# The output layer of a second feed-forward network as Strassen's seven products, with every weight factor streamed from DRAM

## Chip, core and metric

One core of a Trainium2 chip runs the whole program. The metric is device time in microseconds (us); less is better. Times are medians of several executions, and one execution of the kernel before was also profiled.

## What is computed

Three stages follow each other on 2304 tokens (4 batches of 576).

```python
# masked attention, 8 heads of 64: x is [2304, 512]
# first network
h = maximum(maximum(x @ w1, x @ w2), x @ w3)      # [2304, 768]
x2 = h @ w_out                                    # [2304, 512]
# second network
h = x2 @ w_in                                     # [2304, 2048]
g = maximum(h, 0) + alpha * minimum(h, 0)
out = g @ moe2_w_out                              # [2304, 512]
```

The matrix products of the two networks are done in three passes: each operand is split into a high and a low part of a shorter float type, and high x high, high x low and low x high are added up (the table `PAIRS`). So every product below stands for three matmuls.

## The kernel before

**The weave (0 to 324 us).** For batches 0 to 2, attention, the first network and the preparation of weights are tasks with a position; a list scheduler (`Weave.run`) puts them in order by estimated costs. Weights arrive as 64-bit numbers: `from_double` fetches a chunk, a ScalarE and two VectorE instructions (`rebase_words`, `join_words`) make a 32-bit word of it, `split_tasks` makes the two parts. `pair_tasks` does this for eight pairs q of the second network's input weights, forms Strassen's sums of a pair on VectorE (L484) and stores four factor tiles per pair in DRAM. Four chunks of the output weights are prepared and stored there too (`out_chunk_tasks`).

**The last batch of the first network (324 to 400 us)** is written out unit by unit (`first_net`): 36 gate units of 12 matmuls, 8 output units of 18. Beside it `Converter` prepares the other twelve chunks of output weights directly, `load_x2` brings the activations of block 0 back from DRAM, and four of their seven factors are split (`split_x2`).

**The second network (400 us to the end).** The tokens stand in three blocks of 768. A block takes eight steps n, one per pair q. In a step `h_products` computes the pair's hidden values by Strassen's seven products of 6 matmuls with 384 columns each (L814). Two PSUM banks, `ph`, take the products in turn, so a product can start only when VectorE (L819) or ScalarE (L831) has read the one two places ahead of it. `hidden` applies the slope alpha on VectorE (L793, L795) and splits the result (L798 on ScalarE, L801 on VectorE). Between the products stand the output matmuls of the step before: `o_units` yields twelve units of three matmuls with 512 columns (L773), one or two behind each product. They add up in six banks `po` over all 16 chunks. All 16 chunks of output weights stay in SBUF (the pool `wp`); only the input factors (`load_pair`, four tiles per step) come from DRAM. At the block's end `po` is copied and stored. The next block's activations are loaded in step 4 and their factors computed on POOL (L676, L197).

All transfers are issued in program order on one queue, SyncE's (SP). Each engine works its instructions off in the order written.

Of the kernel before, what the change touches and what calls it, by code (L numbers as in the profile page):

```python
# [17 lines left out]
DM = 512  # L18
# [21 lines left out]
DIRECT = 12  # L40
DIRECT_STEPS = tuple(range(4, 28, 2))
LOAD_X, SPLIT_X = 20, 36
# [106 lines left out]
def attention_maxout_prelu_kernel(  # L149
# [59 lines left out]
    od = [dram.tile([P, 2, DM], F32, name=f"wo{f}") for f in range(NF2)]  # L209

    wp = pool(ctx, "wp", NF2)
    wp1 = pool(hx, "wp1", 3 * NF1 + NF1 - NF2)
# [242 lines left out]
    def store_tasks(key, ak, view, n, place, pos, given=None):  # L455

        sk = ("wst", key)
        split_tasks(key, ak, view, n, lambda: wst.tile([P, 2, DM], F32R, tag="w", name="w"), pos,
                    makes=[("wst", sk)], given=given)
        add(load(n), lambda _: nc.sync.dma_start(place[:, :, :n], tl["split", key][:, :, :n].bitcast(F32)),  # L460
            pos, needs=[key], gives=[("stored", key)], uses=[sk])
# [5 lines left out]
    def pair_tasks(q, pos, pace):  # L467
        ek, ok = (from_double(("in", f), w2[f, 0], pos + pace * (f - 2 * q), pace,
                              [("sums", q - 2)] if q > 1 else ())
                  for f in (2 * q, 2 * q + 1))  # L470
        half = DM // 2
        sk = [("word", "sum", q, i) for i in range(2)]
        late = pos + pace

        def sums(_):
            e, a = (tl[k].bitcast(F32) for k in (ek, ok))
            for k in sk:
                tl[k] = words_p.tile([P, DM], U32, tag="word", name="word")
            c, d = (tl[k].bitcast(F32) for k in sk)
            for out_, x, y, op in ((c[:, :half], e[:, :half], a[:, :half], ALU.subtract),  # L480
                                   (a[:, :half], a[:, :half], a[:, half:], ALU.add),
                                   (c[:, half:], a[:, :half], e[:, :half], ALU.subtract),
                                   (d[:, :half], e[:, half:], c[:, half:], ALU.subtract)):
                nc.vector.tensor_tensor(out=out_, in0=x, in1=y, op=op)  # L484

        def whole(a):
            return a

        store_tasks(("h", q, 0), ek, whole, DM, hd[q][0], pos)
        add((dve(half, 4),), sums, late, needs=[ek, ok], gives=[("sums", q)],  # L490
            makes=[("word", k) for k in sk], uses=[ek, ok])
        for i, (k, n) in enumerate(((ok, DM), (sk[0], DM), (sk[1], half))):
            store_tasks(("h", q, i + 1), k, whole if n == DM else lambda a: a[:, :half], n,
                        hd[q][i + 1], late, given=("sums", q))

    def out_chunk_tasks(f, pos, pace):
        ak = from_double(("out", f), w2[f, 1], pos, pace, [("sums", NQ - 1)])
        store_tasks(("o", f), ak, lambda a: a, DM, od[f], pos)

    class Converter:  # L500


        def __init__(self, blocks, raws, floats):
            self.blocks, self.raws, self.floats = list(blocks), raws, floats
            self.sources = [src for src, _ in self.blocks]
            self.fetched, self.line = [], []

        def fetch(self, n=1):
            for src in self.sources[:n]:
                raw = self.raws.tile([P, DM, 2], U32, tag="raw", name="raw")  # L510
                nc.sync.dma_start(raw.rearrange("p n t -> p (n t)"), src.bitcast(U32))
                self.fetched.append(raw)
            del self.sources[:n]

        def steps(self, raw, key):
            a = self.floats.tile([P, DM], U32, tag="word", name="word")
            rebase_words(raw, a)
            yield True
            join_words(raw, a)
            self.fetch()  # L520
            yield True
            t = words[key] = wp.tile([P, 2, DM], F32R, tag="w", name="w")
            nc.scalar.copy(t[:, 0], a.bitcast(F32))
            yield True
            sub(t[:, 1], a.bitcast(F32), t[:, 0].bitcast(F32))

        def step(self, n=1):

            for _ in range(min(n, len(self.blocks))):
                self.line.append(self.steps(self.fetched.pop(0), self.blocks.pop(0)[1]))  # L530
            self.line = [block for block in self.line if next(block, False)]
# [132 lines left out]
    EARLY_X = 4  # L664
    xs, x2h = {}, {}

    def load_x2(blk):

        for i in range(2):
            t = xsp.tile([P, 2, 2, HB], F32, tag="xs", name="xs")  # L670
            for h in range(2):
                nc.sync.dma_start(t[:, :, h, :], x2d[2 * blk + h][:, i::2, :])
            b11, b12, b21, b22 = t[:, 0, 0], t[:, 0, 1], t[:, 1, 0], t[:, 1, 1]
            t2, t3, t4 = (tsp.tile([P, HB], F32, tag="t", name="t") for _ in range(3))
            for out_, x, y in ((t3, b22, b12), (b12, b12, b11), (t2, b22, b12), (t4, b21, t2)):
                nc.gpsimd.tensor_tensor(out=out_, in0=x, in1=y, op=ALU.subtract)  # L676
            for name, x in (("11", b11), ("T1", b12), ("21", b21), ("22", b22), ("T2", t2),
                            ("T3", t3), ("T4", t4)):
                xs[blk, name, i] = x

    def split_x2(blk, k):

        name = PRODUCTS[k][1]
        for i in range(2):
            t = (xmp if k < EARLY_X else xmp1).tile([P, 2, HB], F32R, tag=f"x{k}{i}", name=f"x{k}{i}")
            split(t[:, 0], t[:, 1], xs.pop((blk, name, i)), nc.scalar,
                  nc.gpsimd if blk else nc.vector)
            x2h[blk, k, i] = t

    def load_pair(n):  # L690

        for i in range(4):
            t = words["h", n, i] = (hw1 if n % 3 == 2 else hw).tile([P, 2, DM], F32R, tag="w", name="w")
            m = DM if i < 3 else DM // 2
            nc.sync.dma_start(t[:, :, :m].bitcast(F32), hd[n % NQ][i][:, :, :m])

    def load_out_chunk(f):
        t = words["o", f] = wp.tile([P, 2, DM], F32R, tag="w", name="w")
        nc.sync.dma_start(t.bitcast(F32), od[f])
# [55 lines left out]
    hw1 = pool(ctx, "hw1", 4)  # L755
    xmp1 = pool(ctx, "xmp1", 1)
    gp = pool(ctx, "gp", 8)
    cp = pool(ctx, "cp", 8)
    osp = pool(ctx, "osp", 2)
    ps_h = ctx.enter_context(tc.tile_pool(name="ps_h", bufs=2, space=PSUM, reuse_waits="tile"))  # L760
    ps_o = ctx.enter_context(tc.tile_pool(name="ps_o", bufs=6, space=PSUM, reuse_waits="tile"))
    gts, accs = {}, {}

    def o_unit(n, j, t, first, last):

        blk, q = divmod(n, NQ)
# [8 lines left out]
        if q == NQ - 1 and last:  # L775
            osb = osp.tile([P, DM], F32, tag="osb", name="osb")
# [162 lines left out]
```

## Time and profile before

| | |
|---|---|
| median of 3 runs | 784.21 us (783.13 to 785.36) |
| the profiled execution | 785.25 us, its span 783.5 us |
| TensorE matmul busy, of the span | 760.6 us (97%) |
| VectorE, ScalarE, POOL | 514.6 (66%), 320.5 (41%), 63.1 us (8%) |
| mean granted TensorE clock | 0.992 of full speed |
| bytes moved by DMA | 122.68 MB, mean 157 GB/s |

The span is the time from the first to the last event of the trace. Busy time of matmuls includes overlap of neighbours, so the pace is read from the distance between starts. Of a group of instructions in the timeline the start of the first, the time to the end of the last and the count are given.

### The profile page before, as it was taken

Reading aid. Unit: us, or ns where it says so; the run is one execution under the profiler, and the core shown is the slowest. Engines: PE = TensorE matmul, PEld = TensorE weight load, DVE = VectorE, ACT = ScalarE, POOL = GpSimd, SP = SyncE. Lnnn points to the kernel's source line nnn. Section 1 sums busy time; section 2 is a strip of 40 time slices with the busy share of each in tenths; the row PEclk is TensorE's granted clock in tenths of the full one; section 3 lists DMA queues with packets and bytes.
Section 4 is the critical chain, followed back from the end, with each engine's and each line's share of the span. In section 5 each row is a group of like instructions: output and inputs, shape, how many; then the busy total and the mean of one; then the engine's idle time right before and its main releaser. Section 6 shows DMA issues by size and latency. Waiting matters only on the chain.

```text
span 783.5 us, 13813 instructions
## 1 busy us (share of the span) xinstructions
PE 760.6 (97%) x5056; PEld 705.2 (90%) x5056; DVE 514.6 (66%) x1419; ACT 320.5 (41%) x952; POOL 63.1 (8%) x68
## 2 busy tenths in 40 slices
PE   5899998999999999999999999999999999999997
PEld 4689898999999999999988989998999899989996
DVE  4898998779756243167656677586657677666563
ACT  5997796657755254244421111143111124111112
POOL 1000000000000000002200030071004034000000
PEclk9899999999999999999999999999999999999999
DMA  7577668876761010467363464326454432634002
GB/s 237 156 229 243 213 240 289 284 273 233 265 215 61 1 36 17 151 246 245 111 210 110 126 199 133 94 95 220 144 160 140 120 131 92 211 118 131 1 0 82
DMA packets 51636, 122.68 MB, mean 157 GB/s; under 512 B 7280, under 2 KB 22640, under 8 KB 51568
## 3 DMA queue, kind: packets, MB, share of 16 engines
q1 hardware_dynamic: 51568, 121.79, 46.7%
q8 instruction: 40, 0.66, 0.4%
q14 instruction: 28, 0.23, 0.1%
HBM read 95.56 MB, written 26.21 MB: 155 GB/s over the span
## 4 chain that ended last, share of the span: by engine, by line
PE 84%; DVE 6%; ACT 4%; DMA 4%; issue 1%; SPq 0%; DVEq 0%; ACTq 0%
PE po L773 25%; PE bank L543 22%; PE ph L814 22%; PE bank L565 9%; PE bank L302 2%; PE bank L368 2%; DMA raw<-in_w 2%; PE bank L343 2%; DVE word L431 1%; ACT e L317 1%; DVE word L429 1%; DVE e L310 1%; DMA k<-in_kTs 1%; ACT word L425 1%; DVE w L238 1%
## 5 line engine op out<-in xcount | busy, mean ns | idle before, releaser
L543 PE MATMUL bank<-x,w 128*128 128x288 f32 x1728 | 235.4, 296 | 3.1 <-DVE x L238 2.2
L543 PEld LDWEIGHTS bank<-x,w 128*128 128x128 f32 x1728 | 230.3, 189 | 4.9 <-DVE x L238 2.4
L773 PE MATMUL po<-w,g 128*128 128x512 f32 x864 | 224.8, 392 | 0.0
L814 PE MATMUL ph<-x,w 128*128 128x384 f32 x1008 | 204.1, 337 | 1.3 <-DVE c L819 0.6
L814 PEld LDWEIGHTS ph<-x,w 128*128 128x128 f32 x1008 | 180.5, 188 | 16.8 <-DVE c L819 2.1
L773 PEld LDWEIGHTS po<-w,g 128*128 128x128 f32 x864 | 160.0, 188 | 23.0
L798 ACT CAST g<-neg 128x384 fp32r<-128x384 f32 x96 | 49.4, 514 | 246.1 <-DVE neg L795 246.0
L819 DVE TENSOR_TENSOR c<-ph,c 128x384 f32<-128x384 f32 x168 | 91.1, 554 | 84.3 <-PE ph L814 83.9
L565 PE MATMUL bank<-h,w 128*128 128x288 f32 x576 | 79.5, 297 | 0.0
L801 DVE TENSOR_TENSOR g<-neg,g 128x384 fp32r<-128x384 f32 x96 | 55.3, 576 | 35.0 <-ACT g L798 34.0
L565 PEld LDWEIGHTS bank<-h,w 128*128 128x128 f32 x576 | 76.8, 188 | 1.2 <-issue 0.2
L317 ACT ACTIVATE e<-e,nm 96x128 f32<-96x128 f32 (+2 forms) x176 | 67.8, 392 | 8.6 <-DVE nm L310 8.6
L795 DVE SCALAR_TENSOR_TENSOR neg<-c,neg 128x384 f32<-128x384 f32 x96 | 62.0, 646 | 3.3
L632 DVE TENSOR_TENSOR t<-bank,t 128x288 f32<-128x288 f32 x72 | 32.5, 452 | 37.2 <-PE bank L543 33.7
L238 DVE TENSOR_TENSOR w<-word,w 128x512 fp32r<-128x512 f32 x72 | 47.7, 664 | 13.8 <-ACT w L235 12.2
L676 POOL TENSOR_TENSOR t<-xs 128x384 f32<-128x384 f32 x12 | 14.1, 1178 | 504.5 <-DMA xs<-x 504.1
L793 DVE TENSOR_SCALAR neg<-c,alpha_sb 128x384 f32<-128x384 f32 x96 | 48.8, 508 | 0.9
L425 ACT ACTIVATE word<-raw 128x512 f32<-128x512 f32 x56 | 37.3, 674 | 16.1 <-DMA raw<-in_w 13.4
L431 DVE SCALAR_TENSOR_TENSOR word<-raw,word 128x512 uint32<-128x512 uint32 x56 | 40.2, 717 | 1.9
L235 ACT CAST w<-word 128x512 fp32r<-128x512 f32 (+1 forms) x60 | 35.2, 594 | 13.4 <-DMA wh<-w 10.2
L302 PE MATMUL bank<-k,q 64*96 64x128 f32 (+2 forms) x352 | 29.3, 309 | 6.1 <-DMA k<-in_kTs 6.1
L317 ACT ACTIVATION_READ_ACCUMULATOR e<-e,nm 96x1 f32 (+2 forms) x176 | 34.0, 193 | 0.0
(52 smaller groups left out, 502.7 us busy)
## 6 DMA issues: line engine op xcount, KB each, us to landing
w<-wh SPq DMA_DIRECT2D x72, 512.0 KB, 3.6
raw<-in_w SPq DMA_DIRECT2D x50, 512.0 KB, 4.4
wh<-w SPq DMA_DIRECT2D x24, 512.0 KB, 3.6
w<-wh SPq DMA_DIRECT2D x24, 256.0 KB, 3.0
q<-in_qT SPq DMA_DIRECT2D x16, 288.0 KB, 3.6
xs<-x SPq DMA_DIRECT2D x12, 384.0 KB, 5.8
out_dram<-osb SPq DMA_DIRECT2D x18, 256.0 KB, 2.0
v<-in_vl SPq DMA_DIRECT2D x8, 384.0 KB, 4.1
```

Of the source, the lines that this page charges most:

```text
L238: nc.vector.tensor_tensor(out=out_, in0=x, in1=y, op=ALU.subtract)
L317: nc.scalar.activation(tl[ek][:nq, j, i, :nk], tl[ek][:nq, j, i, :nk], AF.Exp, bias=tl["nm", u][:nq, j, i:i + 1], scale=-1.0, accum_out=tl ...
L431: nc.vector.scalar_tensor_tensor(out=a, in0=raw[:, :, 0], scalar=29, in1=a, op0=ALU.logical_shift_right, op1=ALU.bitwise_or)
L543: nc.tensor.matmul(acc, words["gate", f, g][:, wi, cc * P:(cc + 1) * P], xt[b, cc, hf][:, xi, :], start=n == 0, stop=n == 3 * NCC - 1)
L565: nc.tensor.matmul(acc, words["mix", f][:, wi, dc * P:(dc + 1) * P], st["h", hf, f][:, xi, :], start=n == 0, stop=n == 3 * NF1 - 1)
L773: nc.tensor.matmul(acc, g[:, gi, tt * P:(tt + 1) * P], words["o", 2 * q + j][:, wi], start=q == 0 and first and i == 0, stop=q == NQ - 1 a ...
L793: nc.vector.tensor_scalar(out=neg, in0=h, scalar1=0.0, scalar2=alpha_sb[:, f:f + 1], op0=ALU.min, op1=ALU.mult)
L795: nc.vector.scalar_tensor_tensor(out=neg, in0=h, scalar=0.0, in1=neg, op0=ALU.max, op1=ALU.add)
L798: late.append(lambda: nc.scalar.copy(g[:, 0], neg))
L801: late.append(lambda: nc.vector.tensor_tensor(out=g[:, 1], in0=neg, in1=g[:, 0].bitcast(F32), op=ALU.subtract))
L814: nc.tensor.matmul(bank, words["h", n, i][:, wi, off + c * P:off + (c + 1) * P], x2h[blk, k, c][:, xi, :], start=m == 0, stop=m == 5)
L819: nc.vector.tensor_tensor(out=out_, in0=bank, in1=other, op=ALU.add)
```

## The change

The output layer becomes a Strassen product too. The 16 chunks (the inner dimension) are halved into even and odd, the tokens of a block into two halves of 384, the 512 columns into two of 256. Of the seven products four grow with the pairs: in each step twelve units of three matmuls, now with 256 columns (L790). The other three need sums of hidden values (S1, S3, S4) that are kept in SBUF as plain floats (`kept`, 24 tiles) for the whole block; at its end they are split (`prepare`) and give 3 x 8 x 3 more units, 48 of the last pair's and these before the next block's first step and 36 beside it. Per block that makes 504 output matmuls of 256 columns where 288 of 512 stood.

Around it: all 16 output chunks are prepared in the weave as pairs; 28 factor tiles per block of the output layer are streamed into nine buffers (`load_ow`); the activations' factors of blocks 1 and 2 are computed and split early by `early_x2` on VectorE and ScalarE, stored in DRAM and fetched in a block's last step (`fetch_x2`); those of block 0 are split in the first network's last units; the negative branch of `hidden` moves to ScalarE; POOL has nothing left to do there.

```diff
-DIRECT = 12
-DIRECT_STEPS = tuple(range(4, 28, 2))
-LOAD_X, SPLIT_X = 20, 36
+LOAD_X, SPLIT_X = 33, 36
+NOW = 9
...
-    pace = 3.5
-    for q in range(NQ):
-        pair_tasks(q, NUNITS + 2 * q * pace, pace)
-    for i, f in enumerate(range(DIRECT, NF2)):
-        out_chunk_tasks(f, NUNITS + (2 * NQ + i) * pace, pace)
+    pace = 2.6
+    for s in range(2 * NQ):
+        pair_tasks(s, NUNITS + 2 * s * pace, pace)
...
+    def early_x2(blk, gap=0, rest=0):
+        for i in range(2):
+            rows = load_x2(blk, i, xsp, "xs")
+            for _ in range(1 + gap):
+                yield
+            sum_x2(blk, i, rows, nc.vector)
+            for k in range(7):
+                t = split_x2(blk, k, i, xst, "xst")
+                nc.sync.dma_start(xd[blk][k][i], t.bitcast(F32))
+                for _ in range(1 + rest):
+                    yield
+    def fetch_x2(blk, k):
+        for i in range(2):
+            t = x2h[blk, k, i] = xmp.tile([P, 2, HB], F32R, tag=f"x{k}{i}", name=f"x{k}{i}")
+            nc.sync.dma_start(t.bitcast(F32), xd[blk][k][i])
+    OW = [("o1", q, i) for q in range(NQ) for i in range(2)]
+    OW += [("o2", k, i) for k in range(3) for i in range(NQ // 2)]
...
-        for i, (gi, wi) in enumerate(PAIRS):
-            nc.tensor.matmul(acc, g[:, gi, tt * P:(tt + 1) * P], words["o", 2 * q + j][:, wi],
-                             start=q == 0 and first and i == 0, stop=q == NQ - 1 and last and i == 2)
+    def o_products(g, w, off, t, bank, half, first, last):
+        for i, (gi, wi) in enumerate(PAIRS):
+            nc.tensor.matmul(bank[:, NH * half:NH * (half + 1)], g[:, gi, t * P:(t + 1) * P],
+                             w[:, wi, off:off + NH], start=first and i == 0, stop=last and i == 2)
...
     def hidden(n, j, half, h):
-        neg = cp.tile([P, HB], F32, tag="c", name="neg")
-        nc.vector.tensor_scalar(out=neg, in0=h, scalar1=0.0, scalar2=alpha_sb[:, f:f + 1],
-                                op0=ALU.min, op1=ALU.mult)
-        nc.vector.scalar_tensor_tensor(out=neg, in0=h, scalar=0.0, in1=neg,
-                                       op0=ALU.max, op1=ALU.add)
+        a = acts[j, half] = temp()
+        nc.scalar.activation(a, h, AF.Relu, scale=-1.0)
+        nc.scalar.activation(a, a, AF.Copy, scale=nalpha[:, f:f + 1])
+        def join():
+            nc.vector.scalar_tensor_tensor(out=a, in0=h, scalar=0.0, in1=a, op0=ALU.max, op1=ALU.add)
...
+        def sums():
+            sub_add(s1, a, a22, ALU.add)
+            sub_add(s2, s1, a11)
+            gts[n, 3], lo = split_g(s2)
+            defer(2, lo)
+            def others():
+                sub_add(s3, a11, a)
+                sub_add(s4, a12, s2)
...
+        if blk and q == 0:
+            for i in range(48):
+                next(outs, None)
+            units_before = [5 * i + (i == 7) for i in range(8)]
```

**TensorE, products 1 to 4 of the second step** (`ph` are Strassen products of the hidden layer, `po` output units). Before:

```order
L773 MATMUL po<-w,g 128x512 x3
L814 MATMUL ph<-x_5438,w 128x384 x3
L814 MATMUL ph<-x_5441,w 128x384 x3
L773 MATMUL po<-w,g 128x512 x6
L814 MATMUL ph<-x_5444,w 128x384 x3
L814 MATMUL ph<-x_5447,w 128x384 x3
L773 MATMUL po<-w,g 128x512 x6
L814 MATMUL ph<-x_5450,w 128x384 x3
L814 MATMUL ph<-x_5453,w 128x384 x3
```

Now:

```order
L790 MATMUL po<-w,g 128x256 x3
L947 MATMUL ph<-x_5701,w 128x384 x3
L947 MATMUL ph<-x_5775,w 128x384 x3
L790 MATMUL po<-w,g 128x256 x6
L947 MATMUL ph<-x_5704,w 128x384 x3
L947 MATMUL ph<-x_5778,w 128x384 x3
L790 MATMUL po<-w,g 128x256 x6
L947 MATMUL ph<-x_5707,w 128x384 x3
L947 MATMUL ph<-x_5781,w 128x384 x3
```

The order is the same; the output matmuls between two products have half the columns. What is left of them stands at the block's end.

**VectorE, one step from its second product on.** Before (L819 adds a product up, L793 and L795 are `hidden`, L801 the low part of a split):

```order
L819 TENSOR_TENSOR c<-ph,c 128x384 x2
L793 TENSOR_SCALAR neg<-c,alpha_sb 128x384
L795 SCALAR_TENSOR_TENSOR neg<-c,neg 128x384
L819 TENSOR_TENSOR c<-ph,c 128x384
L801 TENSOR_TENSOR g<-neg,g 128x384
```

Now (L196 is the low part of an early factor, L952 adds a product up, L934 forms the sums of hidden values, L908 joins the branches, L784 is the low part of a split):

```order
L196 TENSOR_TENSOR xst<-t,xst 128x384
L952 TENSOR_TENSOR c<-ph,c 128x384
L934 TENSOR_TENSOR k<-c 128x384
L934 TENSOR_TENSOR c<-k,c 128x384
L952 TENSOR_TENSOR c<-ph,c 128x384
L934 TENSOR_TENSOR k<-c 128x384 x2
L952 TENSOR_TENSOR c<-ph,c 128x384
L784 TENSOR_TENSOR g<-c,g 128x384
L908 SCALAR_TENSOR_TENSOR c<-c 128x384
L952 TENSOR_TENSOR c<-ph,c 128x384 x2
```

Four sums per step came in, four slope instructions (L793) went to ScalarE, and an early factor stands ahead of a product's sum in steps 1 to 7 and 9 to 15.

**SyncE's queue, last step of the first block.** Before, this step issues the four input tiles of the step after next (`wh`), the next step four more, and then come the block's six results:

```order
L695 DMA w<-wh_0_77 128x1024
L695 DMA w<-wh_1_78 128x1024
L695 DMA w<-wh_2_79 128x1024
L695 DMA w<-wh_3_80 128x2x256
L695 DMA w<-wh_0_81 128x1024
L695 DMA w<-wh_1_82 128x1024
L695 DMA w<-wh_2_83 128x1024
L695 DMA w<-wh_3_84 128x2x256
L779 DMA out_dram<-osb 128x512 x6
```

Now the step starts with (`xd` are stored factors of the activations, `xs` activations of block 2, `wp` output factors of the kept products):

```order
L692 DMA x_6914<-xd_0_0_121 128x768
L692 DMA x_6916<-xd_0_1_122 128x768
L657 DMA xs<-x_4_71 128x384
L657 DMA xs<-x_5_72 128x384
L657 DMA xs<-x_4_71 128x384
L657 DMA xs<-x_5_72 128x384
L692 DMA x_6943<-xd_1_0_123 128x768
L692 DMA x_6945<-xd_1_1_124 128x768
L692 DMA x_6965<-xd_2_0_125 128x768
L692 DMA x_6967<-xd_2_1_126 128x768
L700 DMA w<-wh_0_77 128x1024
L700 DMA w<-wh_2_79 128x1024
```

Fourteen fetches of 0.39 MB, four loads of 0.2 MB and two output tiles of 0.52 MB join the four input tiles in this step.

## Rows read from the trace of the kernel before

**Rows 1.** The page's first part: busy time, share of the span, instructions of each engine.

```profile
PE 760.6 (97%) x5056; PEld 705.2 (90%) x5056; DVE 514.6 (66%) x1419; ACT 320.5 (41%) x952; POOL 63.1 (8%) x68
```

**Rows 2.** Busy time by stretch: PE, PEld, DVE, ACT, POOL, then PEclk, DMA share, GB/s.

```profile
100.00:235.00 135.00, 132.78 (x1146) 127.65 (x1145) 107.67 (x391) 91.34 (x308) 0.00 (x0) 0.99 0.74 258
235.00:323.70 88.70, 88.70 (x765) 86.60 (x764) 33.46 (x150) 37.37 (x138) 0.00 (x0) 1.00 0.10 30
323.70:399.90 76.20, 76.20 (x579) 76.20 (x578) 42.97 (x80) 29.22 (x64) 10.11 (x8) 1.00 0.57 196
399.90:411.00 11.10, 9.85 (x51) 8.29 (x50) 9.48 (x20) 4.29 (x10) 0.00 (x0) 1.00 0.87 306
411.00:768.80 357.80, 357.73 (x1783) 322.44 (x1782) 235.43 (x438) 74.04 (x156) 49.74 (x44) 1.00 0.38 122
```

**Rows 3.** Timeline of PE inside a step: start, length, line, count of a group.

```profile
604.44 1.22 PE L814 MATMUL ph<-x,w 128*128 128x384 f32 x6
605.49 0.85 PE L773 MATMUL po<-w,g 128*128 128x512 f32 x3
...
607.23 1.55 PE L773 MATMUL po<-w,g 128*128 128x512 f32 x6
608.62 1.21 PE L814 MATMUL ph<-x,w 128*128 128x384 f32 x6
```

**Rows 4.** Timeline of PE: transposes with a weight load each, and a long run of gates.

```profile
220.54 1.21 PE L343 MATMUL bank<-ident,e 96*128 96x96 f32 x12
221.68 0.71 PE L302 MATMUL bank<-k,q 64*126 64x126 f32 x8
...
242.28 20.79 PE L543 MATMUL bank<-x,w 128*128 128x288 f32 x156
262.92 0.72 PE L343 MATMUL bank<-ident,e 108*108 108x108 f32 x6
```

**Rows 5.** Groups of instructions: count, then busy us, mean ns, idle before.

```profile
L773 PE MATMUL po<-w,g 128*128 128x512 f32 x864 | 224.8, 392 | 0.0
L819 DVE TENSOR_TENSOR c<-ph,c 128x384 f32<-128x384 f32 x168 | 91.1, 554 | 84.3 <-PE ph L814 83.9
L801 DVE TENSOR_TENSOR g<-neg,g 128x384 fp32r<-128x384 f32 x96 | 55.3, 576 | 35.0 <-ACT g L798 34.0
L798 ACT CAST g<-neg 128x384 fp32r<-128x384 f32 x96 | 49.4, 514 | 246.1 <-DVE neg L795 246.0
L795 DVE SCALAR_TENSOR_TENSOR neg<-c,neg 128x384 f32<-128x384 f32 x96 | 62.0, 646 | 3.3
L238 DVE TENSOR_TENSOR w<-word,w 128x512 fp32r<-128x512 f32 x72 | 47.7, 664 | 13.8 <-ACT w L235 12.2
L431 DVE SCALAR_TENSOR_TENSOR word<-raw,word 128x512 uint32<-128x512 uint32 x56 | 40.2, 717 | 1.9
L429 DVE TENSOR_SCALAR word<-word 128x512 uint32<-128x512 uint32 x56 | 24.7, 441 | 7.4 <-ACT word L425 7.4
L484 DVE TENSOR_TENSOR word<-word 128x256 f32<-128x256 f32 x32 | 13.6, 423 | 0.9
```

**Rows 6.** Timeline of DVE: two instructions behind each other in a step.

```profile
422.11 0.56 DVE L819 TENSOR_TENSOR c<-ph,c 128x384 f32<-128x384 f32 x1 [0.50 <-PE ph L814]
422.58 0.55 DVE L801 TENSOR_TENSOR g<-neg,g 128x384 fp32r<-128x384 f32 x1
```

**Rows 7.** Timeline of the first step: a wait of PE, and what DVE did.

```profile
402.18 1.03 DVE L197 TENSOR_TENSOR x<-t,x 128x384 fp32r<-128x384 f32 x2 [0.18 <-ACT x L194]
403.73 2.71 PE L814 MATMUL ph<-x,w 128*128 128x384 f32 x12 [0.56 <-DVE c L819]
```

**Rows 8.** Windows with loads alone in the queue, columns as in Rows 2; then SP's timeline.

```profile
335.00:340.00 5.00, 5.00 (x40) 5.00 (x40) 3.68 (x8) 2.41 (x5) 0.00 (x0) 1.00 1.04 399
405.00:410.00 5.00, 4.31 (x21) 3.36 (x21) 4.67 (x11) 1.02 (x2) 0.00 (x0) 1.00 1.04 413
...
326.32 5.77 SPq L695 DMA_DIRECT2D w<-wh  x8
```

More of the change, by code (lines that the diff above doesn't have):

```diff
@@ L453, in stay_tasks, with store_tasks @@
         split_tasks(key, ak, lambda a: a, DM, tile_of, pos)
-    def store_tasks(key, ak, view, n, place, pos, given=None):
+    def store_tasks(key, ak, n, places, pos, given):
         sk = ("wst", key)
-        split_tasks(key, ak, view, n, lambda: wst.tile([P, 2, DM], F32R, tag="w", name="w"), pos,
+        split_tasks(key, ak, lambda a: a[:, :n], n,
+                    lambda: wst.tile([P, 2, DM], F32R, tag="w", name="w"), pos,
                     makes=[("wst", sk)], given=given)
-        add(load(n), lambda _: nc.sync.dma_start(place[:, :, :n], tl["split", key][:, :, :n].bitcast(F32)),
-            pos, needs=[key], gives=[("stored", key)], uses=[sk])
@@ L467, in pair_tasks @@
-    def pair_tasks(q, pos, pace):
-        ek, ok = (from_double(("in", f), w2[f, 0], pos + pace * (f - 2 * q), pace,
-                              [("sums", q - 2)] if q > 1 else ())
+        for c, place in places:
+            m = place.shape[2]
+            add(load(m), lambda _, c=c, place=place, m=m: nc.sync.dma_start(
+                place, tl["split", key][:, :, c:c + m].bitcast(F32)),
+                pos, needs=[key], gives=[("stored", key)], uses=[sk])
+    def pair_tasks(s, pos, pace):
+        layer, q = divmod(s, NQ)
+        ek, ok = (from_double(("in", layer, f), w2[f, layer], pos + pace * (f - 2 * q), pace,
+                              [("sums", s - 2)] if s > 1 else ())
@@ L484, in sums @@
                 nc.vector.tensor_tensor(out=out_, in0=x, in1=y, op=op)
[L486 to L490, printed above, removed]
+        add((dve(half, 4),), sums, late, needs=[ek, ok], gives=[("sums", s)],
             makes=[("word", k) for k in sk], uses=[ek, ok])
-        for i, (k, n) in enumerate(((ok, DM), (sk[0], DM), (sk[1], half))):
-            store_tasks(("h", q, i + 1), k, whole if n == DM else lambda a: a[:, :half], n,
-                        hd[q][i + 1], late, given=("sums", q))
@@ L496, in out_chunk_tasks @@
[L496 to L531, printed above, removed]
@@ L533, in attention_maxout_prelu_kernel @@
+        for i, k, n, places in parts_:
+            store_tasks(("ho"[layer], q, i), k, n, places, late, ("sums", s))
     PAIRS = ((0, 0), (0, 1), (1, 0))
@@ L781, in o_units, with temp @@
-    def o_units(n):
-        for j, half, last in ((0, 0, False), (1, 0, True), (1, 1, False), (0, 1, True)):
-            for t in range(3 * half, 3 * half + 3):
-                yield o_unit(n, j, t, not last, last)
-    late = []
+    NH = DM // 2
+    nalpha = osp.tile([P, NF2], F32, name="nalpha")
+    nc.vector.tensor_scalar(out=nalpha, in0=alpha_sb, scalar1=-1.0, scalar2=None, op0=ALU.mult)
+    gts, kept, accs, res = {}, {}, {}, {}
+    def temp():
+        return cp.tile([P, HB], F32, tag="c", name="c")
@@ new lines, in sums @@
+        def sums():
+            s1, s3, s4 = kept[1, n], kept[0, n], kept[2, n] = [
+                kp.tile([P, HB], F32, tag="k", name="k") for _ in range(3)]
+            s2 = temp()
+            a11, a12, a22 = acts[0, 0], acts[1, 0], acts[1, 1]
+            sub_add(s1, a, a22, ALU.add)
[5 more added lines that the diff above has]
+                sub_add(s4, a12, s2)
+            defer(1, others)
@@ L804, in h_products, with sub_add @@
+        defer(1, join)
+    def sub_add(out_, x, y, op=ALU.subtract):
+        nc.vector.tensor_tensor(out=out_, in0=x, in1=y, op=op)
     def h_products(n):
         blk = n // NQ
-        banks = [ps_h.tile([P, HB], F32, tag="ph", name="ph") for _ in range(2)]
+        banks = [ps_h.tile([P, DM], F32, tag="ph", name="ph")[:, :HB] for _ in range(2)]
         def product(k, bank):
+            slot[0] += 1
             (i, off), _ = PRODUCTS[k]
@@ L819, in add @@
             nc.vector.tensor_tensor(out=out_, in0=bank, in1=other, op=ALU.add)
-        def rest():
-            while late:
-                late.pop(0)()
-        def temp():
-            return cp.tile([P, HB], F32, tag="c", name="c")
         a, b_ = banks
@@ L831, in h_products @@
         nc.scalar.copy(u, a)
-        rest()
+        due()
         yield
@@ L836, in h_products @@
         add(v, b_, u)
+        due()
         yield
```

298 lines of the change are left out of this document (203 added, 95 removed).

## Prediction, made before the changed kernel was run

> **What bounds the kernel now.** I read the page's first part, then the stretches, then the timelines. Matmuls are busy for 97% of the span [rows 1]; by stretch TensorE has no hole after 235 us except in the first step of the second network [rows 2]. So the time is the number of matmuls times their pace. VectorE is at 80% from 100 to 235 us, 38% from 235 to 324 us and 66% in the second network; the DMA queues fall from 258 to 30 and 122 GB/s in the same stretches [rows 2]. That is room which the change uses up.
>
> The pace must be read from starts, since the mean 392 ns of an output matmul contains overlap [rows 5]. In a step six matmuls of 384 columns take 605.49 - 604.44 = 1.05 us, 0.175 each; six of 512 take 608.62 - 607.23 = 1.39, 0.232 each [rows 3]. 156 gate matmuls of 288 columns take 262.92 - 242.28 = 20.64, 0.1323 each [rows 4]. All stand at a granted clock of 1.00 [rows 2], the level of 2.4 GHz, at which the columns alone take 0.213, 0.160 and 0.120 us. The rest is 12 to 18 ns per matmul and its weight load.
>
> **The output products.** Removed: 864 matmuls of 512 columns. The stretch from 411.0 to 768.8 us [rows 2] holds 23 steps less six matmuls of each kind (2.4 us), so a step takes 360.2 / 23 = 15.66 us and 36 of them in it 15.66 - 42 x 0.175 = 8.31, 0.231 each: 199.4 us in all. Added: 3 x 504 = 1512 of 256 columns, which no row shows. From the gates down by 32 columns at 2.4 GHz gives 0.119; from the 384 row down by 128 gives 0.122; the straight line through the three paces gives 0.118. Above, it can't cost more than the gates' 0.1323. I take 0.120, nearest to the gates' row: 181.4 us. **-18.0 us**, bounds -21.0 to +0.6.
>
> More weight loads come with it, 1512 for 864. Twelve transposes with a load of 128 columns each follow at (221.68 - 220.54) / 12 = 0.095 us [rows 4], so a load every 0.120 us is possible. The Trainium skill ("TensorE: Matmul & The Clock Gate", Part 3) says that a weight load overlaps running matmuls only on another row group; with its load time of 107 ns the two forms would cost, as an estimate, 276 and 323 us, and the change would lose 47. The trace disagrees: by that rule a pair with 512 columns takes 0.320 us, and it takes 0.232 [rows 3].
>
> **The handing over of banks.** A Strassen product needs its bank read by VectorE first. Between a product's end and the second next start stood at least 3 x 0.231 + 1.05 + 6 x 0.231 = 3.1 us; now 0.36 + 1.05 + 0.72 = 2.1. The read takes 0.55 [rows 5], so about 1.3 us are left for what is queued ahead on VectorE. A step now has 19 instructions there (7 adds, 4 joins, 4 sums, 4 low parts); behind each other they start 0.47 us apart [rows 6], 8.9 us of a step of 42 x 0.175 + 36 x 0.120 = 11.7. By their full durations (0.55 to 0.65, [rows 5]) it is 11.0. ScalarE has 13 of about 0.51, 6.6 us. So plain steps are covered. In four steps the early factors of block 2 put four sums and a low part ahead of the second product's add: 5 x 0.47 = 2.3 us more, of which I count 0.4 as a wait of TensorE. **+1.6 us**, bounds 0 to 4.
>
> **The first step** lost 11.1 us for eight products that need 8 x 1.05 = 8.4: there are no output units to stand between, and VectorE was still splitting factors [rows 7]. These splits move into the first network's last units. The chain product, add, join remains. **-1.5 us**, bounds -2.7 to 0.
>
> **The transfers.** Counting the queue's issues, the second network now loads 75 output tiles of 0.52 MB and 28 stored factors beside the same input tiles, and stores factors too: 102.5 MB instead of 48.2. Over some 370 us that is 277 GB/s, against 122 now. The queue carried 399 and 413 GB/s where nothing but loads was waiting [rows 8], and 258 at a share of 0.74, so 349 if full [rows 2]. The last step of a block asks for 9.2 MB in 11.7 us, 26 us of the queue at 349. But 48 units (17 us) stand before the next block's first product, and nine output tiles are loaded ahead, 4.5 steps of them. So I cost the plain steps at nothing, covered by these buffers. A block's end also has a chain: the last hidden values must pass add, two ScalarE instructions, join, two sums and a split (0.2 + 0.55 + 1.0 + 0.65 + 1.1 + 0.5 + 0.6 = 4.6 us from rows 5) before the fourth product's last tiles, which stand 17 units, 6.1 us, later. For both block ends **+2 us**, bounds 0 to 8. If loads are late, the kept products' tiles are late first.
>
> **The weave.** Twelve more chunks and eight pairs are prepared there. The order keeps the early part; they land in 235 to 324 us. VectorE gets 12 x (0.441 + 0.717) + 32 x 0.423 + (24 x 0.664 + 8 x 0.423, a half tile's price taken from L484, - 4 x 0.664) = 44 us more [rows 5], 77 of 88.7 us busy, 87%. From 100 to 235 us, at 80%, TensorE lost 2.2 us [rows 2]. ScalarE gets 40 instructions more, at 0.51 or above [rows 5] at least 21 us, 58 of 88.7. The queue's issues give 19 MB more, 244 GB/s instead of 30. **+1.5 us**, bounds 0 to 5.
>
> **The last batch.** Its twelve preparations go; 28 splits and 16 subtractions come, VectorE's and ScalarE's totals stay near. But the first subtractions stand three units in (4.8 us), and their loads stand behind eight input tiles in the queue, whose issue alone takes 5.8 us [rows 8] and whose 3.7 MB take 9 us more at 399. Both engines wait for them with the gates' reads behind. Eight banks, 12.7 us of gates, cover it just about. **+1 us**, bounds 0 to 5. The end of the program (an add and a store for a copy and a store) stays.
>
> **Sum.** -18.0 + 1.6 - 1.5 + 2 + 1.5 + 1 = -13.4 us. The profiled execution took 785.25 us, 1.0 above the median of the three; I count from the median: 784.2 - 13.4 = **771 us**.
>
> **The rivals.**
> *B, the load sets the pace of short matmuls.* If 256 columns go no faster than the gates' 288, the output costs 1512 x 0.1323 = 200.0 us, no less than before, and the costs around it (+4.6) remain: 789.4 us, slower. It decides from 0.129 us per matmul on. For it: the gates' weight loads are busy all the time, 76.2 of 76.2 us [rows 2]. Against it: 0.095 us of the transposes [rows 4]. The Trainium skill's rule on overlapping loads (the same page and part) is this rival at its extreme.
> *C, the queue doesn't carry it.* If it sustains only the 258 GB/s of the busiest long stretch [rows 2], 102.5 MB take 397 us, 27 more than TensorE's 370: 798 us. It decides below 277 GB/s. For it: stores and loads are mixed, as in that stretch; against it: the share of 0.74 there.
> *D, VectorE's chain paces the steps.* If each of 23 steps loses 0.5 us to adds that come late, that gives back 11.5 us: 782.5, no change. For it: 11.0 of 11.7 us by full durations; against it: starts 0.47 apart.
> *E, the preparation doesn't fit* before the last batch and holds TensorE up by 6 us or more beyond my terms: 777 to 782.
>
> **Chances.** The forecast (765 to 778) 0.66, D 0.15, C 0.08, B 0.07, E 0.04. A measurement can tell 0.3%, 2.4 us. Faster: the forecast, E, D's milder half and some of C, 0.81; the same: most of D's rest and C's edge, 0.07; slower: B and C, 0.12. The range holds the bounds of pace and first step below (784.2 - 21.0 - 1.5 = 762) and reaches to D above: 762 to 784.
>
> **What would show it.** Right: output matmuls start 0.118 to 0.123 apart; a plain step takes 11.7 to 12.0 us; TensorE is without holes from 235 us to the end; the queue is at some 280 GB/s in the second network; weight-load busy time stays below matmul busy time. Wrong: a pace of 0.13 (B); TensorE waiting for tiles `w` or `x` at block ends (C); waits of products for L952 in every step (D); holes between 235 and 345 us (E).

## The result, and the profile after

The changed kernel took **772.26 us** (769.47 to 772.33) against 784.44 us (783.13 to 785.36) for the kernel before beside it: a ratio of 0.9837, 95% interval 0.9811 to 0.9864. Forecast were 771.0, range 762 to 784. The profiled execution took 772.29 us.

The page's first part, for the changed kernel (before: [rows 1]):

```profile
span 770.2 us, 16100 instructions
PE 744.1 (97%) x5704; PEld 723.2 (94%) x5704; DVE 594.6 (77%) x1658; ACT 457.9 (59%) x1238; POOL 3.2 (0%) x16
```

648 more matmuls take 16.5 us less. POOL's work has gone to VectorE and ScalarE.

By stretch, with the columns of [rows 2]:

```profile
100.00:235.00 135.00, 130.12 (x1118) 124.78 (x1117) 110.16 (x383) 92.71 (x303) 0.00 (x0) 0.99 0.79 273
235.00:325.80 90.80, 90.80 (x780) 88.14 (x780) 63.34 (x221) 57.85 (x189) 0.00 (x0) 1.00 0.65 215
325.80:403.20 77.40, 76.43 (x578) 76.20 (x577) 38.07 (x81) 24.72 (x60) 0.00 (x0) 1.00 0.66 235
403.20:412.10 8.90, 8.67 (x50) 8.35 (x49) 5.19 (x11) 4.88 (x10) 0.00 (x0) 1.00 0.57 185
412.10:494.40 82.30, 81.81 (x550) 81.29 (x549) 71.99 (x147) 50.53 (x101) 0.00 (x0) 1.00 0.86 299
494.40:532.00 37.60, 37.03 (x284) 36.36 (x284) 28.11 (x66) 17.27 (x40) 0.00 (x0) 1.00 1.02 392
532.00:738.60 206.60, 205.26 (x1417) 203.57 (x1416) 171.70 (x358) 116.63 (x234) 0.00 (x0) 1.00 0.82 281
```

The first network got longer: the second starts at 403.2 us, not 399.9. The second takes 770.2 - 403.2 = 367.0 us for 383.6. VectorE is busy for 87% of the plain steps (412 to 494 us), and a block's end (494 to 532) drives the queue at 392 GB/s. No matmul of the second network waits for a transfer.

PE's timeline in a plain step (start, length, line, group; a wait in brackets), answering to [rows 3]:

```profile
446.89 1.21 PE L947 MATMUL ph<-x,w 128*128 128x384 f32 x6
...
449.34 0.87 PE L790 MATMUL po<-w,g 128*128 128x256 f32 x6
450.05 1.21 PE L947 MATMUL ph<-x,w 128*128 128x384 f32 x6
...
458.48 0.85 PE L947 MATMUL ph<-x,w 128*128 128x384 f32 x4
```

Six matmuls of 256 columns take 450.05 - 449.34 = 0.71 us, **0.118 each**, and a step takes 458.48 - 446.89 = 11.59 us.

Three places lose time. The first is in the first network:

```profile
218.09 0.96 PE L345 MATMUL bank<-ident,e 96*128 96x96 f32 x9
220.50 0.47 PE L345 MATMUL bank<-ident,e 96*128 96x96 f32 x3 [1.45 <-DVE t L619]
222.05 3.13 PE L530 MATMUL bank<-x,w 128*128 128x288 f32 x12 [1.08 <-ACT pt L237]
```

VectorE's timeline there:

```profile
218.74 1.33 DVE L240 TENSOR_TENSOR w<-word,w 128x512 fp32r<-128x512 f32 x2 [0.36 <-ACT w L237]
219.99 0.45 DVE L619 TENSOR_TENSOR t<-bank,t 128x288 f32<-128x288 f32 x1
```

Two splits of weights (`w`) stand ahead of the maximum (L619) that frees the bank. TensorE stands for 2.5 us, and behind that the granted clock falls:

```profile
222.00:226.00 4.00, 3.95 (x34) 3.79 (x36) 3.97 (x17) 3.95 (x17) 0.00 (x0) 0.64 0.81 239
226.00:230.00 4.00, 4.00 (x36) 3.88 (x33) 2.91 (x11) 2.01 (x8) 0.00 (x0) 1.00 0.84 271
```

A mean of 0.64 is most of four microseconds at 1.2 GHz; then it is 2.4 again. Twelve matmuls take 3.13 us there. The second place is a gate waiting at 346.01 us (below, e7). The third is each block's end, on PE and on its weight loads:

```profile
492.52 2.55 PE L790 MATMUL po<-w,g 128*128 128x256 f32 x17
495.24 2.58 PE L790 MATMUL po<-w,g 128*128 128x256 f32 x16 [0.16 <-DVE g L784]
497.65 2.32 PE L790 MATMUL ph<-w,g 128*128 128x256 f32 x18
...
507.37 4.89 PE L790 MATMUL po<-w,g 128*128 128x256 f32 x36
512.10 1.22 PE L947 MATMUL ph<-x,w 128*128 128x384 f32 x6
```

```profile
494.57 0.30 PEld L790 LDWEIGHTS po<-w,g 128*128 128x128 f32 x2 [0.32 <-ACT g L783]
495.23 1.13 PEld L790 LDWEIGHTS po<-w,g 128*128 128x128 f32 x9 [0.36 <-DVE g L784]
496.71 0.90 PEld L790 LDWEIGHTS po<-w,g 128*128 128x128 f32 x7 [0.35 <-DVE g L784]
...
510.08 1.98 PEld L790 LDWEIGHTS po<-w,g 128*128 128x128 f32 x16 [0.35 <-DVE g L784]
```

150 matmuls take 512.10 - 492.52 = 19.58 us; at 0.118 they would take 17.7. Of the 1.9 us lost, 1.2 lie in the first 33 matmuls (5.13 us to 497.65, for 3.9), and 0.5 in the last 36 (4.73 us from 507.37, for 4.2), where the low part of a kept sum stands on VectorE behind six adds of the drained banks (L794). The hidden values `g` are the weights of these products, so a late low part shows as a wait of the weight load more than of the matmul.

### The profile page after: what moved, and what is told of

Its sections match the earlier page's. It is cut to its first block, busy times and chain, and to the rows that moved or that the text cites. A ratio compares the mean times of both kernels' runs of the same rounds, so it can differ in the third digit from the quotient of the medians.

```text
span 770.2 us, 16100 instructions
## 1 busy us (share of the span) xinstructions
PE 744.1 (97%) x5704; PEld 723.2 (94%) x5704; DVE 594.6 (77%) x1658; ACT 457.9 (59%) x1238; POOL 3.2 (0%) x16
## 4 chain that ended last, share of the span: by engine, by line
PE 60%; DVE 17%; DMA 10%; ACT 8%; issue 3%; SPq 1%; DVEq 0%; ACTq 0%
PE ph L947 20%; PE po L790 15%; PE bank L530 14%; PE bank L552 7%; DMA wh<-w 4%; ACT e L319 2%; DVE word L433 2%; DVE g L784 2%; DMA raw<-in_w 2%; DVE c L794 2%; DVE w L240 2%; PE bank L304 1%; DVE word L431 1%; DVE t L619 1%; PE bank L370 1%
## 5 line engine op out<-in xcount | busy, mean ns | idle before, releaser
L947 PE MATMUL ph<-x,w 128*128 128x384 f32 x1008 | 203.3, 337 | 1.1 <-DVE c L952 1.1
L790 PE MATMUL po<-w,g 128*128 128x256 f32 x1296 | 183.8, 282 | 1.7 <-DVE g L784 0.6
L790 PEld LDWEIGHTS po<-w,g 128*128 128x128 f32 x1296 | 175.5, 189 | 4.2 <-DVE g L784 3.2
L947 PEld LDWEIGHTS ph<-x,w 128*128 128x128 f32 x1008 | 168.3, 188 | 2.1 <-DVE c L952 1.8
L952 DVE TENSOR_TENSOR c<-ph,c 128x384 f32<-128x384 f32 x168 | 90.8, 553 | 33.1 <-PE ph L947 32.2
L783 ACT CAST g<-c 128x384 fp32r<-128x384 f32 x96 | 48.5, 505 | 89.7 <-DVE c L934 56.5
L904 ACT ACTIVATE c<-c 128x384 f32<-128x384 f32 x96 | 50.4, 525 | 34.0 <-DVE c L952 33.0
L237 ACT CAST w<-word 128x512 fp32r<-128x512 f32 x88 | 50.8, 582 | 31.8 <-DMA wh<-w 15.9
L905 ACT ACTIVATE c<-c,nalpha 128x384 f32<-128x384 f32 x96 | 59.2, 617 | 3.1
L908 DVE SCALAR_TENSOR_TENSOR c<-c 128x384 f32<-128x384 f32 x96 | 52.9, 551 | 8.9 <-ACT c L905 8.9
L784 DVE TENSOR_TENSOR g<-c,g 128x384 fp32r<-128x384 f32 x96 | 52.7, 549 | 1.9 <-ACT g L783 1.9
L784 DVE TENSOR_TENSOR g<-k,g 128x384 fp32r<-128x384 f32 x72 | 36.7, 548 | 14.4 <-ACT g L783 14.4
L619 DVE TENSOR_TENSOR t<-bank,t 128x288 f32<-128x288 f32 x72 | 32.3, 449 | 7.6 <-PE bank L530 4.1
L783 ACT CAST g<-k 128x384 fp32r<-128x384 f32 x72 | 33.4, 516 | 7.8 <-PE po L790 4.4
```

Of the source, the lines that this page charges most:

```text
L783: nc.scalar.copy(g[:, 0], x)
L784: return g, lambda: nc.vector.tensor_tensor(out=g[:, 1], in0=x, in1=g[:, 0].bitcast(F32), op=ALU.subtract)
L790: nc.tensor.matmul(bank[:, NH * half:NH * (half + 1)], g[:, gi, t * P:(t + 1) * P], w[:, wi, off:off + NH], start=first and i == 0, stop=l ...
L905: nc.scalar.activation(a, a, AF.Copy, scale=nalpha[:, f:f + 1])
L908: nc.vector.scalar_tensor_tensor(out=a, in0=h, scalar=0.0, in1=a, op0=ALU.max, op1=ALU.add)
L947: nc.tensor.matmul(bank, words["h", n, i][:, wi, off + c * P:off + (c + 1) * P], x2h[blk, k, c][:, xi, :], start=m == 0, stop=m == 5)
```

## The experiments

Theory: at 256 columns the columns still set the pace and the load is hidden; VectorE and the queue have room; the small losses are single waits. Rivals are those of the prediction: B (weight load; e1, e2), C (queue; e4), D (VectorE; e3, e8) and E (preparation; e5, e6).

The runs, each beside its own runs of the kernel before. The last two columns are of the profiled execution: start of the second network (first L947 or its like), and its length.

| run | us, median | ratio, 95% | start | length |
|---|---|---|---|---|
| before | 784.44 | | 399.9 | 383.6 |
| changed | 772.26 | 0.9837 (0.9811 to 0.9864) | 403.2 | 367.0 |
| e1 | 792.75 | 1.0099 (1.0070 to 1.0127) | 397.3 | 390.9 |
| e2 | 970.18 | 1.2364 (1.2298 to 1.2430) | 400.4 | 569.4 |
| e3 | 776.75 | 0.9880 (0.9831 to 0.9930) | 406.4 | 369.8 |
| e4 | 802.42 | 1.0226 (1.0162 to 1.0291) | 405.2 | 392.8 |
| e5 | 770.18 | 0.9825 (0.9794 to 0.9855) | 398.5 | 366.9 |
| e6 | 773.67 | 0.9852 (0.9816 to 0.9889) | 400.5 | 366.9 |
| e7 | 771.75 | 0.9838 (0.9814 to 0.9862) | 402.4 | 367.0 |
| e8 | 771.07 | 0.9839 (0.9783 to 0.9895) | 400.2 | 365.3 |
| e9 | 771.60 | 0.9837 (0.9821 to 0.9854) | 401.8 | 366.9 |
| e10 | 767.52 | 0.9798 (0.9774 to 0.9822) | 400.0 | 365.5 |
| e11 | 767.48 | 0.9786 (0.9764 to 0.9808) | 400.9 | 365.3 |
| e12 | 766.10 | 0.9783 (0.9747 to 0.9818) | 402.3 | 363.3 |

The second network repeats within 0.1 us where nothing in it was edited (changed, e5, e6, e7, e9). The first network, with the changed kernel's order (changed, e3, e4, e8, e9), starts the second anywhere from 400.2 to 406.4 (in e4 the copies begin beside the last batch already). So edits of the second network are judged by its length.

### e1, e2: the pace of short matmuls, without Strassen's method

```diff
-            nc.tensor.matmul(acc, g[:, gi, tt * P:(tt + 1) * P], words["o", 2 * q + j][:, wi],
...
+            for c in range(2):
+                cols = slice(256 * c, 256 * (c + 1))
+                nc.tensor.matmul(acc[:, cols], g[:, gi, tt * P:(tt + 1) * P], words["o", 2 * q + j][:, wi, cols],
...
```

e2 has four pieces of 128.

> The kernel before, each output matmul of 512 columns cut into two of 256, so that 1728 matmuls with their own weight loads do what 864 did; nothing of Strassen's method. My theory (columns set the pace, the load is hidden): 1728 x 0.118 to 0.120 = 204 to 207 us for 199.4, so 4 to 8 us slower than before, 788 to 792; output matmuls start 0.118 to 0.120 apart. Rival B (a load sets the pace of short matmuls, at least 0.129): 223 us or more, 24 us slower, 808 or more.

> The kernel before, each output matmul cut into four of 128 columns, 3456 in all. If the straight line through the paces of 256, 288, 384 and 512 columns goes on (0.118 less 128 columns at 2.4 GHz, 0.0533), they start 0.065 apart: 224 us, 25 us slower than before, 809. Rival (there is a floor, as a 128x128 load needs its own time, and it lies just under 0.118): 0.10 to 0.118 each, 346 to 408 us, 146 to 208 us slower, 930 to 993.

PE's timeline of e1, then of e2:

```profile
606.26 0.87 PE L775 MATMUL po<-w,g 128*128 128x256 f32 x6
606.97 1.22 PE L817 MATMUL ph<-x,w 128*128 128x384 f32 x6
```

```profile
605.12 2.79 PE L775 MATMUL po<-w,g 128*128 128x128 f32 x24
607.75 1.27 PE L817 MATMUL ph<-x,w 128*128 128x384 f32 x6
```

e1: 0.118 each again, and the second network is 7.3 us longer, as the column theory said; the 24 us of rival B did not come. e2: (607.75 - 605.12) / 24 = **0.110**, where the straight line goes on to 0.065: there is a floor, and 0.118 stands 7% above it. So something other than the columns decides below 256 columns. That it is the weight load is not shown: the loads are busy all the time in e1 as well (348.95 of 349.00 us from 411 us on), and the transposes of [rows 4], whose loads have 128 columns too, start 0.095 us apart. The Trainium skill ("TensorE: Matmul & The Clock Gate", "LDWEIGHTS (loading the stationary operand)") gives a load's columns / 1.2 as its time in ns, so as an estimate 107 ns for 128 columns; e2's 0.110 agrees, the 0.095 does not. By the rule of the same page's Part 3, that loads overlap only on another row group, a pair would take, as an estimate, 0.107 + 128 / 2400 = 0.160 us; 0.110 is measured, and that decides.

### e3: is VectorE near its limit?

```diff
-        nc.scalar.activation(a, h, AF.Relu, scale=-1.0)
-        nc.scalar.activation(a, a, AF.Copy, scale=nalpha[:, f:f + 1])
+        nc.vector.tensor_scalar(out=a, in0=h, scalar1=0.0, scalar2=alpha_sb[:, f:f + 1],
+                                op0=ALU.min, op1=ALU.mult)
```

> The changed kernel, with the hidden layer's negative branch on VectorE again (one instruction of 0.518 us in the place of two of ScalarE), so 23 VectorE instructions in a step instead of 19. My theory: VectorE is busy for 72.0 of 82.3 us in plain steps, 10.1 in a step of 11.6; with 4 x 0.518 = 2.1 more it needs 12.2 and becomes the bound of 21 plain steps, 0.6 each, some 13 us slower than the changed kernel, 782 to 788; products wait for the adds in nearly every step. Rival (instructions overlap, 0.47 from start to start, so 10.8 us fit in the step): within 2 us of the changed kernel, 770 to 774, with few waits.

Windows (columns as above), PE's and VectorE's timelines of e3:

```profile
440.00:480.00 40.00, 40.00 (x272) 40.00 (x271) 39.34 (x86) 11.17 (x24) 0.00 (x0) 1.00 0.83 285
```

```profile
446.94 1.22 PE L947 MATMUL ph<-x,w 128*128 128x384 f32 x6
...
458.53 1.21 PE L947 MATMUL ph<-x,w 128*128 128x384 f32 x6
```

```profile
449.22 0.42 DVE L904 TENSOR_SCALAR c<-c,alpha_sb 128x384 f32<-128x384 f32 x1
449.55 0.55 DVE L952 TENSOR_TENSOR c<-ph,c 128x384 f32<-128x384 f32 x1
```

VectorE is busy for 98%, and a plain step still takes 11.59 us. My forecast fell: the added instruction costs 0.33 us to the next start, not 0.518, so a step needs 10.1 + 4 x 0.33 = 11.5 and just fits. The rival's mechanism was right, its total not: 776.75 us lies between the two forecasts. The second network grew by 2.8 us; the later start (406.4 us) is within the scatter of the first network. The first step takes 10.2 us (406.45 to 416.61) for 8.9, and five waits for adds (2.8 us) stand where there were three (1.1 us).

### e4: how much more the queue carries

```diff
             nc.sync.dma_start(t.bitcast(F32), (od1 if which == "o1" else od2)[a][i])
+            spare = dram.tile([P, 2, DM], F32, name=f"spare{len(spares)}")
+            spares.append(spare)
+            nc.sync.dma_start(spare, (od1 if which == "o1" else od2)[a][i])
```

> The changed kernel; behind every load of an output tile the same 0.52 MB are copied within DRAM as well, in the same queue: 75 copies, 39 MB read and 39 written. If the queue has as little room as its busiest plain stretch says (281 GB/s at a share of 0.82, so 343 full), 142 MB read in 367 us (387 GB/s) don't fit: 414 us, some 47 us slower than the changed kernel, 819 or more, TensorE waiting for tiles w and x. If it has the 392 GB/s seen at a block's end, 142 MB take 362 us and it just fits: 772 to 780. If written bytes count as much as read ones, 181 MB take 462 us at 392: 867.

Windows, the waits of PE in the second network, and VectorE ahead of its first step:

```profile
450.00:500.00 50.00, 50.00 (x337) 50.00 (x337) 43.52 (x89) 31.22 (x62) 0.00 (x0) 1.00 1.00 387
560.00:600.00 40.00, 35.77 (x239) 35.22 (x237) 28.58 (x58) 21.49 (x42) 0.00 (x0) 1.00 1.02 406
```

```profile
PE ph L951 <- DMA w<-wh: 7.9, 4, 3.6
PE ph L951 <- DVE c L956: 4.9, 3, 4.1
PE ph L951 <- ACT c L961: 3.1, 1, 3.1
PE po L794 <- DMA w<-wp: 3.0, 2, 1.7
```

```profile
399.95 0.56 DVE L665 TENSOR_TENSOR t<-xs 128x384 f32<-128x384 f32 x1 [5.84 <-DMA xs<-x]
```

Between my cases: the second network is 25.8 us longer. The queue, with loads, stores and copies mixed, goes on at 387 to 413 GB/s, and plain steps at 387 have no hole; only after the first block's end does TensorE wait for tiles (10.9 us in all). Other transfers come late as well. The first step takes 421.37 - 405.25 = 16.1 us for 8.9: block 0's activations (`xs`) arrive late behind the copies, and so do their factors. The wait of 4.1 us for an add (at 604 us) goes back to the late store of an early factor. So 281 GB/s, which the changed kernel needs, is about 70% of what the queue carries, and C is out.

### e5, e6: the pairs' preparation later

```diff
-    pace = 2.6
+    pace = 2.2
...
-        pair_tasks(s, NUNITS + 2 * s * pace, pace)
+        pair_tasks(s, NUNITS + 12 + 2 * s * pace, pace)
```

e6 has 20 and 1.8.

> The changed kernel; the sixteen pairs of second-network weights are due 12 units later in the first network and closer together (2.2 units a chunk for 2.6), so fewer of them meet the attention of the third batch. My theory (the weave loses its time near 220 us, where the pairs' instructions stand ahead of bank-freeing ones on VectorE): the holes of 2.5 us there and the matmuls at a granted clock of 0.64 behind them shrink, the second network starts 2 to 4 us sooner than in the changed kernel (400 to 402 for 403 to 406 us), 768 to 771 in all. Rival (VectorE's total of 87% in the stretch is what counts, wherever the pairs stand): the holes only move, 771 to 775.

> As before, with the pairs due 20 units later and 1.8 units a chunk. My theory: still no loss near 220 us, but the pairs are crowded into 235 to 324 us, where VectorE then has little left: 768 to 773. Rival: the crowding makes new holes there, 774 or more.

PE near 220 us in e5:

```profile
217.44 1.21 PE L345 MATMUL bank<-ident,e 96*128 96x96 f32 x12
219.70 1.88 PE L530 MATMUL bank<-x,w 128*128 128x288 f32 x12 [1.05 <-ACT pt L237]
```

One wait of 1.05 is left of the two, and twelve matmuls take 1.88 us at a clock of 1.00. But the times (770.18 and 773.67) don't set either run apart from the changed kernel by their intervals. And e9, the changed kernel again, had no wait over 0.25 us at this place, and lost 1.6 us between 240 and 320 instead. So the order alone does not fix the hole; that the crowding makes one likely is a guess. In e6 no new hole came either (TensorE is busy for 89.0 of 89.0 us from 235 us on). Whether the pairs' place is worth anything stays open by these two.

### e7, e8: two single waits

e7 issues the first early loads ahead of the eight input tiles:

```diff
+    early = early_x2(1, 2, 1)
+    next(early)
     for n in range(2):
         load_h(n, (0, 2, 1, 3))
-    early = early_x2(1, 2, 1)
```

e8 lets the subtractions of block 2's sums stand behind four products:

```diff
             engine.tensor_tensor(out=out_, in0=x, in1=y, op=ALU.subtract)
+            if spread and out_ is not t4:
+                yield True
...
+            elif more and i % 2 == 0:
+                more = next(early, None)
```

> The changed kernel; in the last batch the loads for block 1's first early sums are issued ahead of the eight input tiles, not behind them. My theory: the single wait of about 1.0 us for a gate's maximum near 346 us, with VectorE waiting 10.6 us for xs before it, goes; the last batch takes 76.2 to 76.6 us instead of 77.4; 771 to 772 in all, at the edge of what the time shows. Rival (the wait is VectorE's own order of work, not the load): it stays.

> The changed kernel; in the second network the four subtractions of block 2's early factors stand one each behind four products of a step, not all four ahead of one add. My theory: the three waits of products for the adds L952 (1.1 us in all, 0.2 to 0.3 us more lost beside each) become none or one, 0.5 to 1.5 us less in the second network (366 for 367 us). Rival (the waits come from the block's end, not from these four): unchanged.

The changed kernel's VectorE and PE near 346 us, and PE at one of e8's waits, first in the changed kernel, then in e8:

```profile
342.79 0.56 DVE L665 TENSOR_TENSOR t<-xs 128x384 f32<-128x384 f32 x1 [10.58 <-DMA xs<-x]
...
346.01 1.19 PE L530 MATMUL bank<-x,w 128*128 128x288 f32 x7 [0.97 <-DVE t L541]
...
428.40 1.33 PE L947 MATMUL ph<-x,w 128*128 128x384 f32 x6 [0.49 <-DVE c L952]
```

```profile
427.90 1.21 PE L953 MATMUL ph<-x,w 128*128 128x384 f32 x6
```

In e7 VectorE waits 1.6 us for `xs`, not 10.6, and no matmul waits from 320 to 400 us; 771.75 us can't show 1 us. The wait for L541 has no fixed size without the edit: 0.97 us in the changed kernel, 0.6, 0.3 and 0.4 in e6, e8 and e9, none in e5. So the edit is worth up to 1 us. In e8 one wait for an add is left, 0.2 us in the first step, and the second network takes 365.3 us: 1.7 less. The mechanism of both theories holds (loads behind loads, four subtractions ahead of one add), and both rivals fall.

### e9 to e11: the edits together

e10 joins e5, e7 and e8. e11 adds one kept sum split ahead:

```diff
-    gp = pool(ctx, "gp", 9)
-    cp = pool(ctx, "cp", 12)
+    gp = pool(ctx, "gp", 10)
+    cp = pool(ctx, "cp", 10)
...
-            for _ in range(2):
+            for _ in range(3):
                 prepare(blk)
```

> The changed kernel once more, beside the next two on the same chip. 770 to 773 us; in the trace a hole near 220 us, the wait for L541 near 346 us and three waits for L952 again, if these belong to the order of the work and not to one execution.

> The changed kernel with the pairs due 12 units later, the early loads ahead of the input tiles and the four subtractions spread. If the three small losses are separate and add up: 1.5 to 2 us near 220 us, 1 us near 346 us, 1.5 us in the second network, so 4 us less than the changed kernel, 767 to 769. Rival (what is taken away in the first network is lost again before it ends, as its weave varies by 2 to 3 us from run to run anyway): 770 to 772.

> As the run with the three edits; besides, at a block's end three kept sums are split ahead of their products instead of two (ten g tiles for nine, ten c tiles for twelve). My theory: the six or seven waits of output products for a low part L784 (0.9 to 1.1 us in all) go, the second network takes 0.5 to 1 us less: 766 to 768. Rival (with ten c tiles the hidden values wait for a free tile): waits for c appear in plain steps, 768 or more.

e9 shows the waits for L541 (0.4 us) and for L952 (three) again, but not the hole near 220 us. e10 is 4.1 us below e9 on the same chip (intervals 0.9774 to 0.9822 and 0.9821 to 0.9854, which just touch), as forecast for all three together. Of the two profiled executions, 1.4 us are the second network's, which repeats; 1.8 are the earlier start, which varies by more than that, so the shares of e5 and e7 are not shown. e11 missed: its second network is 0.2 us shorter. The loss near 507 us is gone, but the last hidden values' high parts now stand behind the third split on ScalarE, 1.7 us of waits for them.

### e12: ready products first

```diff
-            if q == NQ - 1 and k == 3:
+            if q == NQ - 1 and k in (1, 3):
...
-                for p in range(2):
+                for p in ((0, 1) if k == 1 else (2,)):
...
-            for p in range(0 if k else 2, NQ):
+            for p in range(0 if k else 3, NQ):
```

> As the run with three kept sums ahead; besides, at a block's end two kept products run before the last step's second output product and a third before its fourth, so that products which are ready stand before those whose factors come fresh from VectorE and ScalarE. My theory (at each block's end TensorE loses 1 us or more there, as low parts of the last hidden values come late): the 150 output matmuls of a block's end take 18.0 us or less for 19.6 in the changed kernel, the waits for L783 and L784 go, 2 to 3 us less than before this edit, 764.5 to 766. Rival (the late parts are the kept sums themselves, or the next tile's load then waits for a buffer): waits of the same size for kept parts or for tiles w, 767 or more.

PE at the first block's end of e12:

```profile
490.70 1.96 PE L797 MATMUL po<-w,g 128*128 128x256 f32 x15
...
504.37 3.64 PE L797 MATMUL po<-w,g 128*128 128x256 f32 x29
508.73 1.10 PE L797 MATMUL po<-w,g 128*128 128x256 f32 x7 [0.72 <-DVE g L791]
509.67 1.22 PE L954 MATMUL ph<-x,w 128*128 128x384 f32 x6
```

The first 114 matmuls take 504.37 - 490.70 = 13.67 us, 0.120 each: the loss from the fresh low parts is gone. All 150 take 18.97 us, not 18.0, since a kept part is late near the end, behind the six adds of the drained banks again; so the rival has a share here. The second network takes 363.3 us, 2.0 less than e11's; that part is the theory's. The time, 766.1 us, is the lowest of all, but not told apart from e10's and e11's; its interval (0.9747 to 0.9818) lies below that of e9 (0.9821 to 0.9854).

## Why the prediction was right, point by point

The forecast named what bounds the kernel and what the shorter products save. But the sum came out so near partly by luck: two terms missed by 3.0 and 3.7 us in opposite directions.

- **The output products, -18.0.** The pace is 0.118, the straight line's, not the 0.120 that I took: 1512 x 0.118 = 178.4 us for 199.4, -21.0, the bound below. For the same reason a plain step takes 11.59 us, just under the 11.7 to 12.0 that were to show the forecast right.
- **The handing over of banks, +1.6.** 1.4. The four sums stand ahead of an add in two steps, not in four; these lose 0.65 and 0.55 us ahead of a product, and 0.1 on the next. The mechanism is the one named (e8). The figures given there leave 2.1 - 0.55 = 1.6 us ahead of the read, not 1.3.
- **The first step, -1.5.** -2.0 (8.9 us for 10.9). The reason was incomplete: 1.3 us of it come back when the branch returns to VectorE (e3), so the shorter queue there counts too, and perhaps for more than the moved splits.
- **Transfers and block ends, +2.** The step that failed in size: 1.9 us at each of three block ends, 5.7 in all, and none of it a transfer. I let the chain of 4.6 us reach only the fourth product's tiles, 6.1 us off. It is the second and third that come too soon, as nothing else stands ahead of them (1.2 of the 1.9 us; gone in e12). Another 0.5 is the late low part of a kept sum (gone in e11).
- **Weave and last batch, +1.5 and +1.** 3.4 us in the profiled pair. Five starts with the changed order have a mean of 403.4 us, three with the order before (before, e1, e2) of 399.2, so about 4, with a scatter of 3 us to either side. The last batch's 1 us is the load behind eight input tiles, as said (e7), where it comes at all. The place of the weave's loss was wrong: it is before 235 us, where I priced nothing, not in 235 to 324, where TensorE has no hole in the profiled execution. VectorE is busy for 70% there, not the 87% I worked out.
- **The end** was counted at no change. From the last matmul's end to the span's end it is 3.8 us, 1.4 shorter.

-21.0 + 1.4 - 2.0 + 5.7 + 3.4 - 1.4 = -13.9; the spans differ by 13.3. The 0.6 between is less than the rounding of the pace (0.0005 x 1512).

Of the rivals, B is refuted by e1 for 256 columns, C by e4. D's waits are two in the steps, not one in each, and e3 shows how near they are: with 98% a step still holds. The 11.0 of 11.7 us that stood for D used durations of the kernel before, some of them stretched while POOL worked (last section). E's chance was for 6 us beyond my terms; some 1.5 came.

## What to carry to other kernels

Cutting the columns of a matmul pays as long as its pace falls with them: measure the floor (here 0.110 us, met at 128 columns) by cutting an existing product before a method is built on shorter ones. Judge an engine's room by the distance between starts, not by durations. When a scheme puts many products behind one chain at a block's end, put those first whose factors are ready.

## What was not expected of the hardware

- The paces of 256, 288, 384 and 512 columns (0.118, 0.132, 0.175, 0.232 us) lie on one line, and 128 columns (0.110) lie far off it.
- The queue carried 387 to 413 GB/s for long stretches with stores and copies among its loads, as much as the loads alone of [rows 8].
- VectorE's join took 646 ns on average before [rows 5]; on the same shapes it now takes 551 (first line below). The trace of the kernel before shows where the higher mean comes from: a join lasts 1.26 us while POOL works beside it, and 0.56 us while POOL is idle. The add that reads a PSUM bank (L819) keeps its 0.55 us in both. Why POOL's work does this was not tried.

```profile
L908 DVE SCALAR_TENSOR_TENSOR c<-c 128x384 f32<-128x384 f32 x91 | 50.1, 551 | 8.1 <-ACT c L905 8.1
```

The kernel before, POOL and VectorE at 468 us, then VectorE at 483 us:

```profile
468.45 1.02 POOL L676 TENSOR_TENSOR xs<-xs 128x384 f32<-128x384 f32 x1
```

```profile
468.63 1.26 DVE L795 SCALAR_TENSOR_TENSOR neg<-c,neg 128x384 f32<-128x384 f32 x1
...
483.68 0.56 DVE L795 SCALAR_TENSOR_TENSOR neg<-c,neg 128x384 f32<-128x384 f32 x1
```
